# Two early batches as six rows on each of 96 partitions, cast by the load queue, with q transposed on TensorE for batch 0 and by DMA for batch 1

## The chip, the cores and the metric

The kernel runs on one core of one Trainium2 chip. The metric is device time in microseconds (us), and lower is better. Profiles are of one execution; their times count from the start of its span, which is about 1.7 us shorter than the device time of the same execution.

## The reference

```python
# q, k, v: fp32, 8 batches x 8 heads x 576 rows x 64;  w_in 512 x 2048, w_out 2048 x 512
kv  = einsum('bhsd,bhse->bhde', k, v)
o   = einsum('bhsd,bhde->bhse', q, kv)
o   = o / sqrt(mean(o*o, -1) + 1e-6) * g_norm
x   = o.transpose(0, 2, 1, 3).reshape(4608, 512)
h   = x @ w_in
out = (h * sigmoid(1.702 * h)) @ w_out          # fp32
```

## The kernel before

The kernel runs in stages, one dense tile each. Stage t does the dense part of batch t (a hidden half with w_in, then a projection half with w_out) and, in between its matmuls, the attention of batch t + 1. The last stage does the 64 left-over rows of all batches. Units of attention work hang at numbered steps: of 16 groups of the hidden half and of 64 matmuls of the projection half. TensorE takes everything in program order, so a unit that waits holds all that follow: in the profile after, no matmul ran from 42.08 to 46.41 while one `out` waited.

For one batch and each of four pairs of heads: `kv` forms k^T v; q has to come transposed; `out` multiplies it with kv; `ss` sums the squares and `apply` scales. Batches 0 and 1 are special because nothing has been loaded yet. In the kernel before they lie as nine rows on each of 64 partitions and head, two heads stacked, are loaded as fp32 on SyncE's queue (v: cast by GpSimd's), and are cast by three engines into zero-filled block-diagonal tiles. TensorE transposes q with a stacked identity:

```python
def early_load(n, b, c):                       # q and k, fp32
    nc.sync.dma_start(out=staged[b][n][:, c, :], in_=early_src(n, b, c))

class Early(Attention):                        # batches 0 and 1
    def kv(self, c):
        ...
        for j in range(NJ):                    # NJ = 9, zeros in half of kz
            nc.tensor.matmul(t, kz[:, c, j, :], v9[:, c, j * D : (j + 1) * D],
                             start=(j == 0), stop=(j == NJ - 1))
    def q(self, c):
        for j in range(NJ - 1):
            nc.tensor.matmul(t[:, j * R : (j + 1) * R], qz[:, c, j, :], stack, ...)
        nc.vector.tensor_copy(s, t)
...
load_w_in(4, 8); load_w_in(8, 16)              # GpSimd's queue, cast on the way
load_w_out(0, 8); load_w_out(8, 12)
early_load_v(1, 0, 4)
ask_after(0, w_out_sb[:, 7, 0:1])              # batch 1's q and k only when w_out(0, 8) is there
early_stage(1)
for c in range(NPAIR):
    for n in "kq":
        early_load(n, 1, c)
...
# stage 0, projection half, pair c of batch 1
s0 = 14 + 9 * c
at2(s0 - 6, second_casts, c); at2(s0, of(1, "kv", c)); at2(s0 + 2, of(1, "q", c))
at2(s0 + 8, of(1, "out", c)); at2(s0 + 13, of(1, "ss", c)); at2(s0 + 13, of(1, "apply", c))
```

Batches 2 to 7 come in another layout; their q is already transposed by DMA (`qTd`, 512 rows, and `qTr`, the rest), issued from SyncE.

## Time and profile before

| | before |
|---|---|
| device time, median (all its runs) | 301.28 us (299.9 to 302.7) |
| span of the profile | 300.3 us |
| stage 0 begins (hidden half) | 18.85 |
| stage 0, projection half begins | 34.82 |
| stage 1 begins | 53.89 |
| stage 2 begins | 85.92 |
| one later stage | 30.81 |
| granted clock | 1.00 from 7.06 us on; no entry before |

Where the trace has no entry for the clock, the views print 1.00. The head shows that this is no reading: the 12 filler matmuls (matmuls that compute nothing) before 6.5 us step 0.427 us and last up to 634 ns each, those after 8.96 us step 0.22 us and last 379 ns. So TensorE began at about half speed. The lines by stage, and why stages and not busy shares are read, are in the prediction below.

### The profile page before, as it was taken

How to read it: one execution, taken by the hardware profiler on the slowest of the kernel's cores; microseconds unless marked ns; L12 is line 12 of the kernel's file. 1: busy time of each engine (PE TensorE's matmuls, PEld its weight loads, DVE VectorE, ACT ScalarE, POOL GpSimd, SP SyncE). 2: the span in 40 equal slices, each digit the busy share in tenths (PEclk: the TensorE clock that was granted, in tenths of full speed). 3: DMA queues.
4: the chain of work that ended last, by engine and by line, in shares of the span. 5: the costliest groups of instructions: out<-in, count | busy, mean ns of one | idle time of the engine just before them, and what ended most of it. 6: DMA issues, size and time to landing. Idle time of an engine off the chain costs nothing.

```text
span 300.3 us, 3952 instructions
## 1 busy us (share of the span) xinstructions
PE 287.3 (96%) x1549; PEld 135.1 (45%) x1549; DVE 98.0 (33%) x201; ACT 184.0 (61%) x293; POOL 28.7 (10%) x52
## 2 busy tenths in 40 slices
PE   7689989999999999999999999999999999999993
PEld 2334445454445444544444444444454444444441
DVE  5552056262370055214531444134512400110020
ACT  7578757867766775677567756685758666016400
POOL 5550070020012002002000200000000000000000
PEclk9999999999999999999999999999999999999999
DMA  6999994978999992694179507000700030012033
GB/s 144 286 168 196 230 309 145 323 179 238 311 346 252 207 331 101 159 360 87 49 181 326 137 2 219 0 0 2 213 5 2 1 140 2 0 52 87 2 70 70
DMA packets 52531, 44.56 MB, mean 148 GB/s; under 512 B 25120, under 2 KB 47648, under 8 KB 51744
## 3 DMA queue, kind: packets, MB, share of 16 engines
q1 hardware_dynamic: 47584, 38.94, 45.2%
q0 software_dynamic: 4768, 5.37, 11.0%
q8 instruction: 12, 0.20, 0.3%
q14 instruction: 7, 0.06, 0.1%
q10 hardware_dynamic: 160, 0.00, 0.0%
HBM read 36.70 MB, written 9.44 MB: 154 GB/s over the span
## 4 chain that ended last, share of the span: by engine, by line
PE 74%; DMA 18%; DVE 3%; POOL 1%; SPq 1%; issue 1%; ACT 0%; POOLq 0%; DVEq 0%
PE o L369 37%; PE hT L328 30%; DMA qf<-in_q_dram 7%; DMA w_out_sb<-in_moe_w_out_dram 5%; DMA qTd<-qbuf 4%; PE ss L261 2%; DMA kf<-in_k_dram 2%; PE outT L233 2%; PE kvp L202 1%; SPq L93 1%; DVE qbuf L139 0%; DVE kbuf L139 0%; DVE kbuf L101 0%; DVE vbuf L143 0%; POOL kbuf L101 0%
## 5 line engine op out<-in xcount | busy, mean ns | idle before, releaser
L369 PE MATMUL o<-w_out_sb,gT 128*128 128x512 f16 x576 | 137.9, 379 | 0.0
L337 ACT ACTIVATE gT<-hT 128x512 f16<-128x512 f32 x142 | 84.6, 599 | 69.5 <-PE hT L328 69.3
L328 PE MATMUL hT<-xT,w_in_sb 128*128 128x512 f16 x504 | 115.5, 379 | 0.6 <-DVE xT L271 0.5
L369 PEld LDWEIGHTS <-gT 128*128 128x128 f16 x576 | 55.3, 98 | 65.0 <-issue 2.3
L328 PEld LDWEIGHTS <-w_in_sb 128*128 128x128 f16 x576 | 55.2, 98 | 63.3 <-issue 2.2
L271 DVE SCALAR_TENSOR_TENSOR xT<-outT,g_col,rs 128x512 f16<-128x512 f32 x32 | 24.0, 750 | 66.1 <-ACT rs L265 66.1
L377 DVE COPY osb<-o 128x512 f32<-128x512 f32 x34 | 23.3, 685 | 60.7 <-PE o L369 60.7
L263 ACT ACTIVATE ln<-ss,eps_t 128x512 f32<-128x512 f32 (+1 forms) x40 | 25.9, 647 | 18.8 <-PE ss L261 18.7
L265 ACT ACTIVATE rs<-ln 128x512 f32<-128x512 f32 (+1 forms) x40 | 23.5, 589 | 1.3
L253 ACT ACTIVATE sq<-outT 128x512 f16<-128x512 f32 (+1 forms) x40 | 21.7, 542 | 1.7 <-PE outT L233 1.5
L214 DVE CAST kvb<-kvp 64x256 f16<-64x256 f32 x12 | 5.1, 422 | 36.5 <-PE kvp L210 36.4
L261 PE MATMUL ss<-sq,ones 128*128 128x512 f16 (+1 forms) x40 | 14.3, 357 | 0.8 <-ACT sq L253 0.6
L145 POOL CAST krem<-krf 64x512 f16<-64x512 f32 x6 | 4.0, 659 | 112.8 <-DMA krf<-in_k_dram 89.4
L328 PE MATMUL hT<-x_rem,w_in_sb 128*128 128x512 f16 x64 | 14.0, 379 | 0.0
L139 DVE CAST qbuf<-qf 128x512 f16<-128x512 f32 x24 | 10.5, 439 | 2.5 <-DMA qf<-in_q_dram 2.5
L421 PE MATMUL idle<-kvb 128*128 128x512 f16 x29 | 10.1, 483 | 1.2 <-DVE kvb L160 1.2
L139 DVE CAST kbuf<-kf 128x512 f16<-128x512 f32 x24 | 10.5, 438 | 0.0
L337 ACT ACT_TABLE_LOAD x8 | 10.3, 1283 | 0.1
L143 DVE CAST vbuf<-vf 128x512 f16<-128x512 f32 x24 | 10.3, 431 | 0.0
L202 PEld LDWEIGHTS <-kbuf 128*128 128x128 f16 x96 | 7.4, 98 | 5.7
L275 DVE SCALAR_TENSOR_TENSOR x_rem<-outT,g_col,rs 128x256 f16<-128x256 f32 x8 | 3.9, 484 | 17.9 <-ACT rs L265 17.9
L233 PE MATMUL outT<-qTd,kvb 128*128 128x512 f16 x24 | 9.1, 379 | 0.4 <-DMA qTd<-qbuf 0.3
(53 smaller groups left out, 117.9 us busy)
## 6 DMA issues: line engine op xcount, KB each, us to landing
kf<-in_k_dram SPq DMA_DIRECT2D x6, 1024.0 KB, 5.8
vf<-in_v_dram SPq DMA_DIRECT2D x6, 1024.0 KB, 8.8
qf<-in_q_dram SPq DMA_DIRECT2D x6, 1024.0 KB, 11.9
out_dram<-osb SPq DMA_DIRECT2D x6, 1024.0 KB, 3.9
kf<-in_k_dram SPq DMA_DIRECT2D x8, 288.0 KB, 7.2
qf<-in_q_dram SPq DMA_DIRECT2D x8, 288.0 KB, 6.9
out_dram<-osb SPq DMA_DIRECT2D x4, 512.0 KB, 6.0
w_in_sb<-in_moe_w_in_dram POOLq DMA_DIRECT2D x2, 512.0 KB, 6.1
```

The costliest lines, as they stand in the source:

```text
L139: nc.vector.tensor_copy(out=dst[:, c, :, :].rearrange("p j (l d) -> p j l d", l=2), in_=src[n][:, h, :].rearrange("p l (j d) -> p j l d", ...
L202: nc.tensor.matmul(t[:, c, :].rearrange("p (l d) -> p l d", l=2), kh[:, c, j, :], vh[:, 2 * c : 2 * c + 2, j * D : (j + 1) * D], start=(j ...
L233: nc.tensor.matmul(t.rearrange("p c r -> p (c r)"), self.kb[:, c, :], self.qT[c][:, 0:SM], start=True, stop=True,)
L253: nc.scalar.activation(sq[:, 0:n], t, AFT.Square)
L261: nc.tensor.matmul(t[:, 0:n], ones2, sq[:, 0:n], start=True, stop=True)
L263: nc.scalar.activation(ln[:, 0:n], t[:, 0:n], AFT.Ln, bias=eps_t, scale=1.0 / D)
L265: nc.scalar.activation(rs[:, 0:n], ln[:, 0:n], AFT.Exp, bias=0.0, scale=-0.5)
L271: nc.vector.scalar_tensor_tensor(self.x[:, c, :], o, g_col, rs, op0=ALU.mult, op1=ALU.mult)
L328: nc.tensor.matmul(h, w_in_sb[:, ko, fo * P : (fo + 1) * P], x[:, ko, :], start=(ko == 0), stop=(ko == KO - 1),)
L337: nc.scalar.activation(gT[:, fo, :], h, AFT.Gelu_apprx_sigmoid)
L369: nc.tensor.matmul(os[mo], gT[:, fo, mo * P : (mo + 1) * P], w_out_sb[:, fo, :], start=(fo == 0), stop=(fo == FO - 1),)
L377: (nc.scalar.copy if deep and mo % 2 else nc.vector.tensor_copy)(osb[:, mo, :], os[mo])
```

## The change

The intent: spare the zero fills and the casts of the early batches by letting the load queue cast, spare TensorE work by packing two heads side by side in the array (64-column tiles, batch 0) or in one 128-column matmul (batch 1), and take batch 1's q off TensorE by a DMA transpose. The diff, cut to its core:

```diff
-    def early_load(n, b, c):
-        nc.sync.dma_start(out=staged[b][n][:, c, :], in_=early_src(n, b, c))
+    def early_load(n, b, c0, c1):                     # q, k, v; PE_ = 96, NJ = 6
+        nc.gpsimd.dma_start(
+            out=raw[n][0:PE_, c0:c1, :].rearrange("p c (l x) -> p (c l) x", l=2),
+            in_=early_src(n, b, c0, c1),
+        )
 ...
-        for c in range(NPAIR):                        # casts of batches 2 to 7
-            for n, dst in (("k", kh), ("q", qh)): ...
-            nc.vector.tensor_copy(out=vh[:, h, :], in_=src["v"][:, h, :])
+        for n, dst in (("q", qh), ("k", kh), ("v", vh)):
+            for c in range(NPAIR): ...
 ...
-    class Early(Attention):
+    class First(Attention):
         def kv(self, c):
+            for j in range(NJ):
+                for hl in range(2):
+                    nc.tensor.matmul(t[hl * D : (hl + 1) * D, :],
+                                     kraw[0:PE_, c, x], vbuf[0:PE_, c, x], ...)
         def q(self, c):
+            for j in range(NJ):
+                for hl in range(2):
+                    nc.tensor.transpose(t[hl * D : (hl + 1) * D, j * PE_ : (j + 1) * PE_],
+                                        qraw[0:PE_, c, ...], ident[0:PE_, 0:PE_])
+    class Second(Attention):
+        def transpose_q(self):
+            s = attn.tile([P, NPAIR * NJ, PE_], F16, name="qTe", tag="qTe", bufs=1)
+            nc.sync.dma_start_transpose(out=s, in_=qbuf[0:PE_, :])
 ...
     load_w_in(8, 16)
     load_w_out(0, 8)
+    early_load("q", 1, 0, 4)
+    early_load("k", 1, 0, 4)
+    early_load("v", 1, 0, 4)
     load_w_out(8, 12)
-    early_load_v(1, 0, 4)
-    ask_after(0, w_out_sb[:, 7, 0:1])
-    ... batch 1's q and k on SyncE's queue ...
+    load_w_out(12, 16)
 ...
+            at1(14, of(1, "pack_q"))
+            at1(14, of(1, "transpose_q"))
             for c in range(NPAIR):
-                ... (casts, kv, q, out, ss, apply at 14 + 9 * c and after)
+                at2(6, of(1, "pack_k", c))
+                at2(18 + c, of(1, "kv", c))
+                at2(27 + 8 * c, of(1, "out", c))
+                at2(34 + 8 * c, of(1, "ss", c))
+                at2(34 + 8 * c, of(1, "apply", c))
```

Not shown: q and k of batch 0's first pair still come as fp32 on SyncE's queue; 8 filler matmuls (matmuls that compute nothing) open the head instead of 12; the output of batches 0 and 1 is stored in eight pieces instead of two; kv of later batches comes one group later.

More of the change, by code (lines that the diff above doesn't have):

```diff
@@ L6 @@
 from concourse._compat import with_exitstack
-from concourse.masks import make_identity
 F16 = mybir.dt.float16
@@ L42 @@
     NT = B + 1
-    NJ = S // R
     EARLY = 2
+    PE_ = 96
+    NJ = S // PE_
+    assert PE_ * NJ == S and PE_ % 32 == 0
     const = ctx.enter_context(tc.tile_pool(name="const", bufs=1))
@@ L66 @@
     qbuf = const.tile([P, NPAIR * NJ * P], F16)
-    vbuf = const.tile([P, NPAIR * NJ * D], F16)
+    kraw = const.tile([P, NPAIR, 2 * NJ * D], F16)
+    qraw = const.tile([P, NPAIR, 2 * NJ * D], F16)
+    vbuf = const.tile([P, NPAIR, 2 * NJ * D], F16)
     ident = const.tile([P, P], F16)
-    stack = const.tile([P, D], F16)
     ones2 = const.tile([P, P], F16)
     eps_t = const.tile([P, 1], F32)
-    zero_t = const.tile([P, 1], F16)
     g_col = const.tile([P, 1], F32)
@@ L76, with early_src, pack @@
     x_rem = const.tile([P, KO, B * R], F16)
-    kz = kbuf.rearrange("p (c j e) -> p c j e", c=NPAIR, j=NJ)
-    qz = qbuf.rearrange("p (c j e) -> p c j e", c=NPAIR, j=NJ)
-    v9 = vbuf.rearrange("p (c x) -> p c x", c=NPAIR)
-    def early_stage(b):
-        staged[b] = {
-            n: stage.tile([P, NPAIR, NJ * D], F32, name=f"{n}f", tag=f"{n}f") for n in "kq"
-        }
-    def early_src(n, b, c):
-        return srcs[n][b, 2 * c : 2 * c + 2].rearrange("l (p j) d -> (l p) (j d)", j=NJ)
-    def early_load(n, b, c):
-        nc.sync.dma_start(out=staged[b][n][:, c, :], in_=early_src(n, b, c))
-    def early_load_v(b, c0, c1):
-        src = v[b, 2 * c0 : 2 * c1].rearrange("(c l) (p j) d -> (l p) c (j d)", l=2, j=NJ)
-        nc.gpsimd.dma_start(out=v9[:, c0:c1, :], in_=src)
-    def early_cast(b, c, n, hl, copy):
-        r = slice(hl * D, (hl + 1) * D)
-        copy(
-            out=(kz if n == "k" else qz)[r, c, :, r],
-            in_=staged[b][n][r, c, :].rearrange("p (j d) -> p j d", d=D),
+    raw = {"k": kraw, "q": qraw, "v": vbuf}
+    def early_src(n, b, c0, c1):
+        return srcs[n][b, 2 * c0 : 2 * c1].rearrange("h (p j) d -> p h (j d)", j=NJ)
+    def early_load(n, b, c0, c1):
[3 more added lines that the diff above has]
+        )
+    def pack(n, dst, c):
+        nc.vector.tensor_copy(
+            out=dst[0:PE_, c * NJ * P : (c + 1) * NJ * P].rearrange(
+                "p (j l d) -> p j l d", j=NJ, l=2
+            ),
+            in_=raw[n][0:PE_, c, :].rearrange("p (l j d) -> p j l d", l=2, j=NJ),
         )
@@ L108 @@
     qh = qbuf[:, 0 : NPAIR * SM].rearrange("p (c j e) -> p c j e", c=NPAIR, j=J)
-    vh = vbuf[:, 0 : NPAIR * SM].rearrange("p (h x) -> p h x", h=H)
+    vh = vbuf.rearrange("p c x -> p (c x)")[:, 0 : NPAIR * SM].rearrange("p (h x) -> p h x", h=H)
     def load_batch(b):
@@ L113, in load_batch @@
         for n in "kvq":
-            if n == "v":
-                t = stage.tile([P, NPAIR * SM], F32, name="vf", tag="vf")
-            else:
-                t = stage.tile([P, NPAIR, NJ * D], F32, name=f"{n}f", tag=f"{n}f")
-                t = t.rearrange("p c x -> p (c x)")[:, 0 : NPAIR * SM]
-            t = tiles[n] = t.rearrange("p (h x) -> p h x", h=H)
+            t = tiles[n] = stage.tile([P, H, J * D], F32, name=f"{n}f", tag=f"{n}f")
             nc.sync.dma_start(
@@ L135, in casts @@
         src = staged[b]
-        for c in range(NPAIR):
-            h = slice(2 * c, 2 * c + 2)
-            for n, dst in (("k", kh), ("q", qh)):
-                nc.vector.tensor_copy(
-                    out=dst[:, c, :, :].rearrange("p j (l d) -> p j l d", l=2),
-                    in_=src[n][:, h, :].rearrange("p l (j d) -> p j l d", j=J),
-                )
-            nc.vector.tensor_copy(out=vh[:, h, :], in_=src["v"][:, h, :])
+        for n, dst in (("q", qh), ("k", kh), ("v", vh)):
+            for c in range(NPAIR):
+                h = slice(2 * c, 2 * c + 2)
+                if n == "v":
+                    nc.vector.tensor_copy(out=vh[:, h, :], in_=src["v"][:, h, :])
+                else:
+                    nc.vector.tensor_copy(
+                        out=dst[:, c, :, :].rearrange("p j (l d) -> p j l d", l=2),
+                        in_=src[n][:, h, :].rearrange("p l (j d) -> p j l d", j=J),
+                    )
@@ L144, in casts @@
         for n, t in (("kr", krem[b % 2][0:R]), ("vr", vrem[b % 2][0:R]), ("qr", qrem[b % 2])):
             nc.gpsimd.tensor_copy(out=t.rearrange("p c (l d) -> p (c l) d", l=2), in_=src[n])
+    first = {}
+    for n in "qk":
+        first[n] = stage.tile([P, H, J * D], F32, name=f"{n}f", tag=f"{n}f")
+        first[n] = first[n].rearrange("p h x -> p (h x)")[0:PE_, 0 : 2 * NJ * D]
+        nc.sync.dma_start(
+            out=first[n].rearrange("p (h x) -> p h x", h=2), in_=early_src(n, 0, 0, 1)
+        )
@@ L148 @@
     for hl in range(2):
         nc.scalar.dma_start(out=g_col[hl * D : (hl + 1) * D, :], in_=g_norm.unsqueeze(1))
-    early_stage(0)
-    for c in range(NPAIR):
-        for n in "kq":
-            early_load(n, 0, c)
-    early_load_v(0, 0, 1)
-    early_load_v(0, 1, 2)
-    make_identity(nc, ident)
-    early_load_v(0, 2, 4)
-    nc.vector.memset(zero_t, 0.0)
-    nc.vector.memset(kvb[1], 0.0)
-    nc.scalar.preload_act_table_set("natural_log_exp_and_others")
-    for c in range(NPAIR):
-        nc.vector.memset(kz[:, c], 0.0)
-        nc.scalar.copy(
-            qz[:, c].rearrange("p j e -> p (j e)"), zero_t.to_broadcast([P, NJ * P])
-        )
-        if c == 0:
-            nc.vector.memset(ones2, 0.0)
-            nc.vector.memset(ones2[0:D, 0:D], 1.0)
-            nc.vector.memset(ones2[D:P, D:P], 1.0)
-            nc.vector.tensor_add(stack, ident[:, 0:D], ident[:, D:P])
-            nc.vector.memset(eps_t, EPS)
@@ L173 @@
-    nc.vector.memset(kvb[0], 0.0)
+    nc.vector.memset(ident, 0.0)
+    nc.vector.memset(kvb[1], 0.0)
+    early_load("v", 0, 0, 1)
+    nc.gpsimd.affine_select(
+        out=ident,
+        in_=ident,
+        compare_op=ALU.not_equal,
+        fill=1.0,
+        base=0,
+        pattern=[[-1, P]],
+        channel_multiplier=1,
+    )
+    for c in range(1, NPAIR):
+        for n in "qkv":
+            early_load(n, 0, c, c + 1)
+    nc.scalar.preload_act_table_set("natural_log_exp_and_others")
@@ L176, in load_w_in @@
+    nc.vector.memset(ones2, 0.0)
+    nc.vector.memset(ones2[0:D, 0:D], 1.0)
+    nc.vector.memset(ones2[D:P, D:P], 1.0)
+    nc.vector.memset(eps_t, EPS)
     def load_w_in(f0, f1):
@@ L211, in kv, with keep_kv @@
             if c == NPAIR - 1:
-                for hl in range(2):
-                    r = slice(hl * D, (hl + 1) * D)
-                    nc.vector.tensor_copy(self.kb[r, :, r], t[r, :, r])
+                self.keep_kv()
+        def keep_kv(self):
+            for hl in range(2):
+                r = slice(hl * D, (hl + 1) * D)
+                nc.vector.tensor_copy(self.kb[r, :, r], self.kvp[r, :, r])
         def transpose_q(self):
@@ L282, in apply @@
                 )
-    class Early(Attention):
+    class First(Attention):
         def kv(self, c):
-            pool, tag = (ps_o, "o") if self.b == 0 else (ps_a, "att")
-            t = pool.tile([P, D], F32, name="kv9", tag=tag)
+            t = ps_o.tile([P, D], F32, name="kv0", tag="o")
             for j in range(NJ):
-                nc.tensor.matmul(
-                    t,
-                    kz[:, c, j, :],
-                    v9[:, c, j * D : (j + 1) * D],
-                    start=(j == 0),
-                    stop=(j == NJ - 1),
-                )
+                for hl in range(2):
+                    x = slice((hl * NJ + j) * D, (hl * NJ + j + 1) * D)
+                    nc.tensor.matmul(
+                        t[hl * D : (hl + 1) * D, :],
+                        kraw[0:PE_, c, x],
+                        vbuf[0:PE_, c, x],
+                        start=(j == 0),
+                        stop=(j == NJ - 1),
+                    )
             nc.vector.tensor_mul(
@@ L302, in q @@
         def q(self, c):
-            t = ps_h.tile([P, SM], F32, name="q9", tag="hT")
-            for j in range(NJ - 1):
-                nc.tensor.matmul(
-                    t[:, j * R : (j + 1) * R], qz[:, c, j, :], stack, start=True, stop=True
-                )
-            s = attn.tile([P, SM], F16, name="qT", tag="qT", bufs=4)
+            t = ps_h.tile([P, S], F16, name="q0", tag="hT")
+            for j in range(NJ):
+                for hl in range(2):
+                    nc.tensor.transpose(
+                        t[hl * D : (hl + 1) * D, j * PE_ : (j + 1) * PE_],
+                        qraw[0:PE_, c, (hl * NJ + j) * D : (hl * NJ + j + 1) * D],
+                        ident[0:PE_, 0:PE_],
+                    )
@@ L309, in q, with rest, pack_q, pack_k @@
+            s = attn.tile([P, S], F16, name="qT", tag="qT", bufs=4)
             nc.vector.tensor_copy(s, t)
             self.qT[c] = s
-        def q_rest(self):
-            t = ps_a.tile([P, NPAIR, R], F32, name="q9r", tag="att")
+        def rest(self, c):
+            return self.qT[c][:, SM:S]
+    class Second(Attention):
+        def pack_q(self):
             for c in range(NPAIR):
-                nc.tensor.matmul(t[:, c, :], qz[:, c, NJ - 1, :], stack, start=True, stop=True)
-            self.qr = attn.tile([P, NPAIR, R], F16, name="qrT", tag="qrT", bufs=1)
-            nc.vector.tensor_copy(self.qr, t)
+                pack("q", qbuf, c)
+        def pack_k(self, c):
+            pack("k", kbuf, c)
+        def kv(self, c):
+            if c == 0:
+                self.kvp = ps_a.tile([P, NPAIR, P], F32, name="kvp", tag="att")
+            t = self.kvp
+            v2 = vbuf[0:PE_, c, :].rearrange("p (l x) -> p l x", l=2)
+            for j in range(NJ):
+                nc.tensor.matmul(
+                    t[:, c, :].rearrange("p (l d) -> p l d", l=2),
+                    kbuf[0:PE_, (c * NJ + j) * P : (c * NJ + j + 1) * P],
+                    v2[:, :, j * D : (j + 1) * D],
+                    start=(j == 0),
+                    stop=(j == NJ - 1),
+                )
+            if c == NPAIR - 1:
+                self.keep_kv()
+        def transpose_q(self):
+            s = attn.tile([P, NPAIR * NJ, PE_], F16, name="qTe", tag="qTe", bufs=1)
+            nc.sync.dma_start_transpose(out=s, in_=qbuf[0:PE_, :])
+            s = s.rearrange("p (c j) r -> p c (j r)", c=NPAIR)
+            for c in range(NPAIR):
+                self.qT[c] = s[:, c, 0:SM]
+            self.qTe = s
@@ L319, in rest @@
         def rest(self, c):
-            return self.qr[:, c, :]
+            return self.qTe[:, c, SM:S]
     def dense(t, units1, units2, group, deep):
@@ L381, in project @@
                         if 2 * mo + g < EARLY:
-                            rows = rows.rearrange("(p j) m -> p j m", j=NJ)[:, NJ - 1, :]
+                            p0 = SM % PE_
+                            rows = rows[bass.DynSlice(NJ * p0 + SM // PE_, R, step=NJ), :]
                         else:
@@ L395, in dense @@
         if t < EARLY:
-            rows = out[t * S : (t + 1) * S, :].rearrange("(p j) m -> p j m", j=NJ)
-            for g in range(2):
+            n = 0
+            while n < SM:
+                mo, j, p = n // P, n // PE_, n % PE_
+                m = min((mo + 1) * P, (j + 1) * PE_) - n
                 nc.sync.dma_start(
-                    out=rows[:, bass.DynSlice(g, NPAIR, step=2), :],
-                    in_=osb[g * R : (g + 1) * R, :, :],
+                    out=out[t * S : (t + 1) * S, :][bass.DynSlice(NJ * p + j, m, step=NJ), :],
+                    in_=osb[n % P : n % P + m, mo, :],
                 )
+                n += m
         elif t < B:
@@ L405, in dense @@
             )
-    a0 = Early(0)
-    def first_casts(c):
-        early_cast(0, c, "k", 0, nc.vector.tensor_copy)
-        early_cast(0, c, "k", 1, nc.gpsimd.tensor_copy)
-        early_cast(0, c, "q", 0, nc.vector.tensor_copy if c == 3 else nc.gpsimd.tensor_copy)
-        early_cast(0, c, "q", 1, nc.gpsimd.tensor_copy if c == 2 else nc.scalar.copy)
+    a0 = First(0)
+    nc.scalar.copy(qraw[0:PE_, 0, :], first["q"])
+    nc.vector.tensor_copy(kraw[0:PE_, 0, :], first["k"])
     idle_ps = ps_h.tile([P, SM], F32, name="idle", tag="hT")
@@ L427, in busy @@
             )
-    first_casts(0)
-    busy(12)
+    busy(8)
     for c in range(NPAIR):
+        a0.q(c)
         a0.kv(c)
-        a0.q(c)
         if c:
             a0.ss(c - 1)
-        if c == 1:
-            load_w_in(0, 4)
-        if c + 1 < NPAIR:
-            first_casts(c + 1)
         busy(2)
@@ L445 @@
             busy(3)
+    load_w_in(0, 4)
     load_w_in(4, 8)
@@ L448 @@
     load_w_out(0, 8)
+    early_load("q", 1, 0, 4)
+    early_load("k", 1, 0, 4)
+    early_load("v", 1, 0, 4)
     load_w_out(8, 12)
-    early_load_v(1, 0, 4)
-    after = const.tile([P, 2], F32)
-    def ask_after(i, landed):
-        nc.gpsimd.tensor_copy(after[:, i : i + 1], landed)
-        nc.sync.dma_start(out=after[0:D, i : i + 1], in_=g_norm.unsqueeze(1))
-    ask_after(0, w_out_sb[:, 7, 0:1])
-    early_stage(1)
-    for c in range(NPAIR):
-        for n in "kq":
-            early_load(n, 1, c)
-    def second_casts(c):
-        early_cast(1, c, "k", 0, nc.vector.tensor_copy)
-        early_cast(1, c, "k", 1, nc.gpsimd.tensor_copy)
-        early_cast(1, c, "q", 0, nc.gpsimd.tensor_copy)
-        early_cast(1, c, "q", 1, nc.scalar.copy)
-        if c == 0:
-            load_w_out(12, 16)
+    load_w_out(12, 16)
+    after = const.tile([1, 1], F32)
     def third():
-        ask_after(1, w_out_sb[:, FO - 1, 0:1])
+        nc.gpsimd.tensor_copy(after, w_out_sb[0:1, FO - 1, 0:1])
+        nc.sync.dma_start(out=after, in_=g_norm[0:1].unsqueeze(1))
         load_batch(2)
@@ L479, in start @@
     def start(b):
-        live[b] = Early(b) if b < EARLY else Attention(b)
+        live[b] = Second(b) if b == 1 else Attention(b)
     for t in range(NT):
@@ L497 @@
             at1(("ko", 1), of(0, "apply", NPAIR - 1))
-            at1(4, of(0, "q_rest"))
-            at1(6, of(0, "out", NPAIR))
+            at1(4, of(0, "out", NPAIR))
             at2(4, of(0, "ss", NPAIR, True))
@@ L504 @@
                 at1(8, nc.vector.memset, r[R:P], 0.0)
+            at1(14, of(1, "pack_q"))
+            at1(14, of(1, "transpose_q"))
             for c in range(NPAIR):
-                s0 = 14 + 9 * c
-                at2(s0 - 6, second_casts, c)
-                at2(s0, of(1, "kv", c))
-                at2(s0 + 2, of(1, "q", c))
-                at2(s0 + 8, of(1, "out", c))
-                at2(s0 + 13, of(1, "ss", c))
-                at2(s0 + 13, of(1, "apply", c))
-            at2(s0, third)
+                at2(6, of(1, "pack_k", c))
[3 more added lines that the diff above has]
+                at2(34 + 8 * c, of(1, "apply", c))
+            at2(14, third)
         elif b < B:
             if t == 1:
-                at1(3, of(1, "q_rest"))
                 at2(46, of(1, "out", NPAIR))
@@ L526 @@
             for c in range(NPAIR):
-                at1((11 if t == 1 else 8) + c, of(b, "kv", c))
+                at1((11 if t == 1 else 9) + c, of(b, "kv", c))
             for c in range(NPAIR + 1):
```

## The prediction

> **What bounds the kernel now.** I read the shares first, then the table by stage, then the chain of waits, and last the DMA rate in short stretches. One core is in use and the granted clock is 1.00 throughout, so clock plays no part.
>
> ```profile
> PE 287.3 (96%) x1549; PEld 135.1 (45%) x1549; DVE 98.0 (33%) x201; ACT 184.0 (61%) x293; POOL 28.7 (10%) x52
> ```
>
> TensorE looks full, but a 128x512 matmul counts 379 ns busy while a run of them steps much faster (in the chain, 64 take 13.81 us, so 0.216 us each). Holes under 0.16 us are therefore hidden, and filler matmuls (10.1 us in the head) count as work. So I time stages by their boundaries: from 18.85 (first dense matmul), 34.82, 53.89, 85.92, 117.00 on.
>
> ```profile
> 18.85:34.82 15.97, 14.95 (x75) 6.68 (x74) 3.01 (x7) 12.99 (x22) 0.53 (x2) 1.00 1.18 202
> 34.82:53.89 19.07, 17.80 (x142) 9.00 (x141) 9.94 (x18) 13.18 (x21) 6.21 (x10) 1.00 0.83 242
> 53.89:85.92 32.03, 31.72 (x172) 15.09 (x171) 13.16 (x26) 23.23 (x39) 3.76 (x6) 1.00 0.99 268
> 85.92:117.00 31.08, 30.97 (x163) 14.63 (x161) 10.84 (x23) 20.75 (x34) 3.03 (x6) 1.00 0.94 241
> 117.00:147.81 30.81, 30.81 (x163) 14.65 (x161) 10.84 (x23) 20.64 (x33) 1.51 (x3) 1.00 0.59 169
> ```
>
> Columns: stretch, length, busy time of PE, weight load, DVE, ACT, POOL, clock, DMA share, GB/s. Steady state is 30.81: 128 dense matmuls (27.63) and 3.18 of attention for the next batch. From 117.00 to the end nothing can be gained. The head, stage 0 (19 + 35 us) and stages 1 and 2 hold everything: what can move is the moment at which stage 2 begins, 85.92, plus its 0.27 us hole. What sets 85.92 is in the chain of waits:
>
> ```profile
> 3.19 10.09 DMA qf<-in_q_dram
> ...
> 16.80 14.95 DMA w_out_sb<-in_moe_w_out_dram
> ...
> 32.70 5.97 DMA kf<-in_k_dram
> ...
> 49.13 11.93 DMA qf<-in_q_dram
> ...
> 65.66 4.39 DMA qTd<-qbuf
> 70.09 0.38 PE outT L233
> ```
>
> Start, length, what. Until 70.09 the chain is nearly all DMA; TensorE takes over only there. By 46.9, when the last of w_out lands, the queues have read three tensors twice (8x8x576x64 fp32 = 3.54 MB a batch) and two weights of 4.19 MB, 15.47 MB: 344 GB/s from 2 us on. How far that is from what the engines can do:
>
> ```profile
> 2.00:7.00 5.00, 4.52 (x11) 1.46 (x10) 2.83 (x9) 4.99 (x5) 2.96 (x6) 1.00 0.81 182
> 16.00:18.00 2.00, 1.69 (x21) 1.00 (x21) 2.00 (x4) 1.92 (x4) 2.00 (x4) 1.00 0.66 69
> 26.00:34.00 8.00, 8.00 (x43) 3.68 (x41) 1.05 (x4) 5.80 (x11) 0.19 (x1) 1.00 1.23 205
> 37.00:42.00 5.00, 3.73 (x33) 1.76 (x31) 2.79 (x5) 2.17 (x4) 3.04 (x5) 1.00 1.03 397
> 42.00:47.00 5.00, 5.00 (x54) 2.80 (x53) 3.29 (x8) 3.84 (x7) 2.98 (x5) 1.00 0.75 128
> 66.80:70.00 3.20, 3.00 (x22) 1.54 (x21) 0.84 (x2) 1.79 (x3) 0.00 (x0) 1.00 0.96 184
> ```
>
> GB/s counts bytes written, so a casting load at 205 reads 410. Full rate is about 400 read (26 to 34; uncast 397 at 37 to 42). The first five microseconds, 16 to 18 (weights asked for late, GpSimd being busy with casts) and 42 to 47 run below it.
>
> [...]
>
> **The change part by part.**
> Head. Zero fills (4 DVE at 0.54, 4 ACT at 1.15 us) and batch 0's 16 casts go, except one ACT and one DVE copy of pair 0. kv costs 12 small matmuls a pair in place of 9, q 12 in place of 8; both were about 0.25 us. None of this bounds: pairs arrive at the pace of DMA, 0.885 MB each, 2.3 us at 385. I take 385 for 1536-byte rows, between 348 for 1024-byte rows (50 to 59 us) and 400. Reading from 2.0 on, [...] batch 0 ends at [...] 11.9; before, the last q landed at 13.28. GpSimd no longer casts, so weights follow with no hole: w_in and half of w_out, 6.29 MB at 405, 15.5 us, end 27.4; before, 31.75. TensorE: first dense matmul near 15.5 instead of 18.85 (when the first 1 MB of w_in lands), projection from about 31 instead of 34.82.
> Batch 1 loads. 3.54 MB at 385, 9.2 us. Into the same stretch falls the new transpose of 96x3072 f16, 0.59 MB. The old pair of transposes, likewise 0.59 MB, took most of 66.8 to 70 (0.96 x 3.2 = 3.1 us of all engines); I take 2.75. v lands last: 27.4 + 9.2 + 2.75 [...] = 40.1. TensorE reaches its place, projection step 18, at 31 + 18 x 0.216 = 34.9, and waits about 5 us, where it now waits 1.27 before kv.
> From there: 46 steps (9.93), kv 24 x 0.055 = 1.3, four out and four ss, 1.7: stage 1 begins 13.0 after v, at 53.1 (53.89 before). Removed from TensorE in stages 0 and 1: kv 1.04 + q 0.96 + rest of q 0.28, less 1.3 for the new kv, so 1.0 us.
> Stage 1. The rest of w_out, 2.1 MB at 405, ends 5.2 us after v, 45.3 (46.9 before). Batch 2 is requested behind it and follows the old pattern (46.9 to q landed at 61.06, 14.2): 59.5. But casts now run q, k, v. Transposes gain: they start after 4 casts, not 11. kv loses: it needs 9 casts before its first pair, at 0.335 each plus about 1 us of the slowing seen at 61.8 to 63.9 (0.84 instead of 0.42): 4.0, so kv at 63.5. By its own path TensorE reaches it at 53.1 + 3.5 (grouped part) + 8 x 0.863 = 63.5: both arrive together. Then 5 hidden groups and kv (5.35), 64 projections with out and ss (16.0): stage 2 at 84.9 instead of 85.92.
> Stage 2. Earlier transposes remove its 0.27 hole. The eight output pieces instead of two cost SyncE queue time that I expect to be covered.
> Sum: -1.0 (stage 2's start) - 0.27 = -1.3: 300.0. I shade it to 299.6, because each lag that the two paths share (385 against a possible 410 for batch loads) errs on the slow side.
>
> **The rivals.**
> (a) TensorE sets the pace, and its savings count in full: head 3.3, the wait before kv 1.3, holes of stage 0 (1.1), stage 1 (0.9), work 1.0: up to 7 us, 294. For it: the page's 96%. Against it: the chain, DMA until 70; the same bytes have to be read. It would need batch 2's q landed before 55; 15.47 MB at 405 alone ends at 40.2 from 2.0, and 14.2 more is 54.4, with no start, latency or transpose. I give it 4%.
> (b) Nothing gained: the new transpose eats what the closed holes give (2.75 against about 4), batch 2's q lands at 61 as before, and kv, now behind 9 casts, starts at 65.1 instead of 64.64: 301.5. [...] For it: DMA stays saturated. Against: slack at 16 to 18 and 42 to 47 is real.
> (c) Batch loads run at 410 and the transpose hides in gaps: v at 37, stage 2 near 82.5: 297.5.
> (d) Requests from GpSimd, 96-row tiles [...] run slower than 385, say 330: each batch costs 1.5 us more, 302.5. Nine requests at 0.75 us feed 0.295 MB each, 393 GB/s, so there is little to spare at the start.
>
> **Range and chances.** Between (b) and (c) lies most of it: 297.2 to 301.5 holds 8 in 10, centre 299.6. Two per cent faster is 295.3 or less, only through (a): 0.04. Slower by over 2% is above 307, for which several of (d) and the clock must meet: 0.02. Within 2%: 0.94.
>
> **What would show it right or wrong.** In the changed kernel's chain: DMA of batch 1's v, then of batch 2's q or its casts, ahead of TensorE. First dense matmul at 15 to 16. TensorE waiting 3 to 6 us at kvp in stage 0, on the DMA of v. Bytes read near 400 GB/s from 4 to 27 us without a hole. The table by stage: stage 2 begins at 84 to 86, all later stages 30.81. I am wrong if v lands before 36, if the transpose takes little from the loads, if the wait at step 18 lowers the granted clock, or if stage 2 shows a longer wait for its transpose because eight output pieces hold SyncE's queue.

Two terms of its sum go with that, an allowance for the start of the loads and one for their landing: what is left of it, 2.0 + 9.2 for batch 0, 15.5 for the weights, 9.2 + 2.75 for batch 1, puts v at 38.65, where the author's sum came to 40.1 and went on from there to 300.0, shaded to 299.6. The 330 of rival (d) is a supposition, not a reading. That GB/s counts bytes written is seen in the page of before: GpSimd's casting loads read 10.7 MB of fp32 and stand there with 5.37 MB (q0).

## More of the kernel before

The kernel before took 299.9 to 302.7 us over all its runs here, so differences of a few tenths are read from stage lengths in a profile and not from one time.

## The result, and the profile after

The changed kernel is correct and slower: 306.42 us median (306.17 to 306.66, four runs) against 301.59 (301.13 to 302.17) for the kernel before in the same session. The ratio is 1.0159, interval 1.0137 to 1.0181. The predicted range, 297.2 to 301.5, missed it.

The table by stage of the changed kernel, with the columns of the table in the prediction (stretch, length, busy time of PE, weight load, DVE, ACT, POOL, clock, DMA share, GB/s):

```profile
16.48:32.22 15.74, 14.85 (x72) 6.57 (x72) 2.59 (x6) 12.75 (x22) 3.50 (x5) 1.00 1.22 207
32.22:58.81 26.59, 20.23 (x99) 8.98 (x97) 6.41 (x15) 10.09 (x17) 0.38 (x2) 0.87 1.11 229
58.81:90.54 31.73, 31.51 (x168) 14.93 (x167) 11.97 (x25) 23.46 (x39) 2.97 (x6) 1.00 1.01 273
90.54:121.30 30.76, 30.76 (x163) 14.59 (x161) 11.86 (x23) 20.71 (x34) 3.58 (x6) 1.00 0.67 173
```

Stage by stage against the table of before: the head is 2.37 us shorter (16.48 against 18.85), the hidden half of stage 0 0.23 shorter, stage 1 0.30 and stage 2 0.3 shorter. One half-stage is 7.52 longer: the projection half of stage 0, 26.59 instead of 19.07. Of the stages in the table it is also the only one whose clock is not 1.00. The whole loss sits there. What TensorE waited for, in us in total, times, longest:

```profile
PE outT L231 <- DMA qTe<-qbuf: 4.3, 1, 4.3
PE kvp L335 <- DMA vbuf<-in_v_dram: 2.0, 1, 2.0
```

And the chain of waits of the changed kernel there (start, length, what):

```profile
17.70 15.94 DMA vbuf<-in_v_dram
33.64 12.64 DMA qTe<-qbuf
46.41 0.58 PE outT L231
46.99 2.99 PE o L403 x7
```

The new transpose of batch 1's q was issued at 33.64 and landed at 46.27. TensorE came to the first `out` of batch 1 at about 42 and stood until 46.41. Then seven projection matmuls took 2.99 us where seven take 1.51 elsewhere. The clock explains that; here are three single microseconds of the changed kernel, in the same columns:

```profile
44.00:45.00 1.00, 0.00 (x0) 0.00 (x0) 0.00 (x0) 0.00 (x0) 0.00 (x0) 0.96 1.27 108
47.00:48.00 1.00, 1.00 (x3) 0.29 (x2) 0.00 (x0) 0.60 (x1) 0.00 (x0) 0.50 0.67 178
51.00:52.00 1.00, 1.00 (x4) 0.39 (x3) 0.17 (x1) 0.97 (x3) 0.00 (x0) 0.62 1.09 366
```

TensorE idles, the granted clock (third number from the end) falls to 0.50 at 44.93, and it is 1.00 again only from 51.76 on. The first line holds a second fact: at 44 to 45 the DMA engines are fully busy (1.27) but write only 108 GB/s. So why did 0.59 MB take 12.6 us? The share of each DMA queue from 40 to 42 (queue, packets, MB written, share of 16 engines; q0 is GpSimd's queue with the casting loads, q1 SyncE's with the transpose):

```profile
q0 software_dynamic: 308, 0.31, 90.8%
q1 hardware_dynamic: 308, 0.08, 29.6%
```

The packet counts are equal. A load packet writes 1 KB (2 KB of fp32 read), a transpose packet 256 B, and so the transpose gets a fifth of the bytes. From 45 to 46, when the loads are through, it gets 615 packets in one microsecond.

These equal turns are seen from 37.6 to 42.5 only, 5 of the 12.6 us. From its issue at 33.64 until 37.60 no transpose packet moved at all. And from 42.5 to 45, with few load packets left, the transpose still crept. The queues from 44 to 45:

```profile
q1 hardware_dynamic: 399, 0.10, 123.0%
q0 software_dynamic: 7, 0.01, 3.7%
```

That is 49 ns of an engine a packet (1.23 x 16 us over 399) where it took 31 ns in the turns and 18 ns from 45 on, after the last load packet had ended at 44.72. Why it crept, and why it started so late, no run shows. Without the loads both are much shorter: in `e1_quiet` the first packet came 1.3 us after the issue, and only 35.0 to 35.5 was slow (112 packets).

The half-stage adds up so: 64 projection matmuls 13.81, rest of batch 0's ss 0.11, kv 24 x 0.055 = 1.32, four out 0.86, four ss 0.86, together 16.96. The wait for v is 2.2 by the pitch of 0.216 (the views count a matmul as busy for 379 ns where a run steps by 216, hence 2.0), the one for the transpose 4.5. That leaves 26.59 - 16.96 - 6.7 = 2.9, mostly the clock.

### The profile page after: what moved, and what is told of

The parts are those of the page before. It is cut to its first block, busy times and chain, and to the rows that moved or that the text cites. A ratio compares the mean times of both kernels' runs of the same rounds, so it can differ in the third digit from the quotient of the medians.

```text
span 304.8 us, 3833 instructions
## 1 busy us (share of the span) xinstructions
PE 288.7 (95%) x1521; PEld 134.1 (44%) x1521; DVE 87.7 (29%) x187; ACT 175.2 (57%) x283; POOL 23.9 (8%) x43
## 4 chain that ended last, share of the span: by engine, by line
PE 84%; DMA 11%; ACT 2%; DVE 1%; issue 1%; POOL 0%; POOLq 0%
PE o L403 39%; PE hT L362 36%; DMA vbuf<-in_v_dram 7%; DMA qTe<-qbuf 4%; PE ss L259 3%; PE outT L231 2%; PE kvp L197 2%; PE idle L456 1%; ACT ln L261 1%; ACT rs L263 1%; PE kvp L205 0%; PE hO L362 0%; PE q L307 0%; ACT osb L411 0%; PE outT L242 0%
## 5 line engine op out<-in xcount | busy, mean ns | idle before, releaser
L403 PE MATMUL o<-w_out_sb,gT 128*128 128x512 f16 x576 | 139.4, 383 | 0.0
L403 PEld LDWEIGHTS <-gT 128*128 128x128 f16 x576 | 56.2, 99 | 67.4 <-issue 4.9
L212 DVE CAST kvb<-kvp 64x256 f16<-64x256 f32 x14 | 5.9, 422 | 50.1 <-PE kvp L205 46.1
L456 PE MATMUL idle<-kvb 128*128 128x512 f16 x25 | 9.1, 492 | 1.3 <-DVE kvb L149 1.3
L131 DVE CAST kbuf<-kf 128x512 f16<-128x512 f32 x24 | 9.6, 460 | 0.0
L197 PE MATMUL kvp<-vbuf,kbuf 128*128 128x128 f16 x96 | 9.3, 219 | 0.0
L129 DVE CAST vbuf<-vf 128x512 f16<-128x512 f32 x24 | 8.5, 416 | 0.0
```

The costliest lines, as they stand in the source:

```text
L197: nc.tensor.matmul(t[:, c, :].rearrange("p (l d) -> p l d", l=2), kh[:, c, j, :], vh[:, 2 * c : 2 * c + 2, j * D : (j + 1) * D], start=(j ...
L403: nc.tensor.matmul(os[mo], gT[:, fo, mo * P : (mo + 1) * P], w_out_sb[:, fo, :], start=(fo == 0), stop=(fo == FO - 1),)
L456: nc.tensor.matmul(idle_ps, kvb[1][:, 0, :], kvb[1].rearrange("p c r -> p (c r)"), start=True, stop=True,)
```

## The experiments

Theory A: the transpose is not slow, it starves beside the casting loads, which share the engines with it packet by packet; its wait brings the half clock with it. Theory B: the transpose is slow in itself (96 rows, 3072 columns, or SyncE's 8.07 us of issuing it). Theory C: something else in the change costs (96-row loads, small tiles, output pieces).

**The transpose with the engines to itself** (`e1_quiet`). The k and v of batch 1 and the last half of w_out are asked for after it has landed.

```diff
     early_load("q", 1, 0, 4)
-    early_load("k", 1, 0, 4)
-    early_load("v", 1, 0, 4)
-    load_w_out(8, 12)
-    load_w_out(12, 16)
+    def rest_of_loads():                      # called right after transpose_q
+        nc.gpsimd.tensor_copy(landed, live[1].qTe[0:1, 0, 0:1])
+        ... the four loads ...
```

> The changed kernel, but k and v of batch 1 and the last half of w_out are asked for only when the transpose of q has landed, so the transpose has the DMA engines to itself. Theory A (the transpose starves behind the casting loads of GpSimd's queue): it lands 4 to 6 us after its issue, like the transposes of later batches (5.4), instead of 12.6. Theory B (96 rows or 3072 columns are slow as such, or SyncE's 8 us of issuing them): 11 to 13 us again. The total gets longer in both, 308 to 313, because 4.5 MB of loads come later; it is not the point.

Measured: 311.51 us, one run. The transpose's own lines in this run (issue: duration in ns and start; then us from issue to landing):

```profile
L347 SPq DMA_TRANSPOSE qTe<-qbuf x1: 3785/3785/3785, 33.0 to 33.0; - x1
DMA to landing us min/median/max: 5.1/5.1/5.1
```

It lands in 5.1 us instead of 12.6, with the same rows, columns and engine, and SyncE issues it in 3.79 us instead of 8.07: the long issue went with the loads beside it. B falls. The rest of the loads then came too late (10.4 us of waiting for v), as intended.

**Filler in the hole** (`e2_fill`).

```diff
+            at2(27, fill, 20)     # 20 matmuls into a spare PSUM tile, ahead of out(1, 0)
```

> The changed kernel with 20 useless matmuls (20 x 0.216 = 4.3 us) put just before the first out of batch 1, in the hole in which TensorE waits for the transpose. The wait itself stays: the transpose lands at 46.3 as before. Theory: the half clock from 45 to 51.4 follows from the idle time and costs about 2.5 us beside the wait's 4.3: with the hole filled the clock stays 1.00 and the time is 303.6 to 304.2. Rival (the clock falls for another reason, or the loads and not TensorE set the end): 306.4.

Measured: 304.13 us (303.87 to 304.55), ratio to before 1.0100 (1.0062 to 1.0138). The same kind of single microseconds as above:

```profile
44.00:45.00 1.00, 1.00 (x7) 0.47 (x5) 0.00 (x0) 0.00 (x0) 0.00 (x0) 1.00 1.27 80
47.00:48.00 1.00, 1.00 (x7) 0.41 (x6) 0.00 (x0) 0.49 (x1) 0.00 (x0) 1.00 0.45 144
```

The transpose landed at 46.3 as before, 12.8 us after its issue. The clock stays at 1.00, seven matmuls run in the microsecond from 47 instead of three, and the span falls from 304.8 to 302.4. So of the loss 2.3 to 2.4 us is the clock that follows the wait, got back by work that computes nothing.

**q of batch 1 asked for earlier** (`e4_q_early`).

```diff
+    early_load("q", 1, 0, 4)
     load_w_out(0, 8)
-    early_load("q", 1, 0, 4)
```

> The changed kernel with batch 1's q asked for before the first half of w_out, so its transpose is issued about 5 us earlier, near 28.5. Theory A, starving until the casting queue is empty near 43: it still lands at 44 to 46, the wait shrinks by 0 to 2 us, 304 to 306.5. Theory B, a fixed 12.6 us: it lands at 41, no wait at out, no half clock, 299 to 300.

Measured: 304.89 us (304.60 to 305.48), ratio to before 1.0126 (1.0087 to 1.0165). Waits of TensorE, and the transpose's time to landing:

```profile
PE kvp L335 <- DMA vbuf<-in_v_dram: 5.1, 1, 5.1
PE outT L231 <- DMA qTe<-qbuf: 0.4, 1, 0.4
```

```profile
DMA to landing us min/median/max: 18.7/18.7/18.7
```

Issued at 29.0 instead of 33.6, the transpose landed at 47.7 instead of 46.3. A fixed duration of 12.6 is refuted once more. The wait moved: beside the transpose the loads fell from about 205 GB/s written to 145 to 155, and from 38.0 to 38.5 both queues all but stood (32 GB/s); v came at 42.4, not 38.6. I had expected the wait to stay at `out`; the time lay in the range, the place did not.

**q of batch 1 on TensorE** (`e3_te_q`), straight from the cast rows as for batch 0.

```diff
-            at1(14, of(1, "pack_q"))
-            at1(14, of(1, "transpose_q"))
+            q = First.q; rest = First.rest            # in class Second
             for c in range(NPAIR):
-                at2(6, of(1, "pack_k", c))
+                at2(5 + 3 * c, of(1, "q", c))
+                at2(16, of(1, "pack_k", c))
```

> The changed kernel with batch 1's q transposed on TensorE as batch 0's is, straight from the cast rows (48 small matmuls, about 1.2 us), so no DMA transpose in stage 0. If the transpose is the whole loss: no wait at out, no half clock, v lands near 38 and TensorE waits 1 to 2 us there, stage 2 begins at 82 to 84, 297 to 299. If something else in the change costs (96-row loads, small tiles, output pieces, order of casts): above 301.

Measured: 300.77 us (300.49 to 300.94), ratio to before 0.9987 (0.9942 to 1.0031): 5.65 us faster than the changed kernel in the medians, level with the kernel before. The longest waits of TensorE:

```profile
PE kv L290 <- DMA vbuf<-in_v_dram: 1.7, 1, 1.7
PE q L307 <- DVE qT L313: 1.3, 1, 1.3
```

No wait for a transpose, none for v of batch 1, clock 1.00 throughout stage 0, stage 2 at 84.63. It is slower than the 297 to 299 expected, because of the second line, a wait that I made: the copy of the first q out of PSUM stood on VectorE behind batch 0's last `apply`. C is refuted as the cause of the loss: the rest of the change, all of it still in, is no slower than before.

**The same with q's groups moved** (`e6_q_placed`), at steps 1, 3, 12 and 15.

```diff
-                at2(5 + 3 * c, of(1, "q", c))
+                at2((1, 3, 12, 15)[c], of(1, "q", c))
```

> Batch 1's q on TensorE, with its four groups of transposes at projection steps 1, 3, 12 and 15 in place of 5, 8, 11 and 14. In the run before, the second group waited 1.27 us for the first one's copy, which stood on VectorE behind batch 0's last apply. With the first two copies ahead of it that wait goes: stage 2 begins 1.0 to 1.3 us earlier, 299.3 to 300.0. Rival, v of batch 1 now lands too late and takes over the wait: 300.5.

Measured: 299.34 us (299.19 to 299.52), ratio to before 0.9939 (0.9906 to 0.9973). Stage 2 begins at 83.30; the waits of TensorE from 20.5 us on are gone but for 0.2. This is the fastest version. Run again in five rounds (`e6_again`, same kernel):

> The fastest version so far once more, in the same rounds as the one above, to place it against the kernel before: 0.6% faster, 299.1 to 299.8.

Measured: 299.98 us (299.83 to 300.98), ratio 0.9967 (0.9944 to 0.9990). That is just above the 299.8 expected. So it beats both kernels, by 0.3 to 0.6% the kernel before. In the profile of this repeat TensorE waited 1.8 us for the first part of w_in, which it had not done in the first; loads vary by that much from run to run.

**Four transposes instead of one** (`e5_split`), each a pair's 768 columns.

```diff
-            nc.sync.dma_start_transpose(out=s, in_=qbuf[0:PE_, :])
+            for c in range(NPAIR):
+                nc.sync.dma_start_transpose(
+                    out=s[:, c * NJ : (c + 1) * NJ, :],
+                    in_=qbuf[0:PE_, c * NJ * P : (c + 1) * NJ * P])
```

> The changed kernel with batch 1's q transposed by four DMA requests, one a pair, in place of one. In the trace of the changed kernel, packets of the two queues alternate one for one (308 and 308 in two microseconds), a transpose packet carrying 256 B and a load packet about 1 KB written. If that stays, 0.17 MB of transposes are through by 42, so pair 0 (0.15 MB) lands near 41, in time for its out at 42.1, and the others near 43.5, 44.5 and 46, each about when its out comes (8 steps apart): no long wait, clock 1.00, 299 to 301. Rival, the transposes as a whole land only when the casting queue is empty: pair 0 lands after 44, wait over 2 us, 303 to 306.

Measured: 301.77 us (300.36 to 302.24), ratio to before 1.0004 (0.9957 to 1.0051). The waits of TensorE have no line for the transpose. The two longest are:

```profile
PE kvp L335 <- DMA vbuf<-in_v_dram: 2.4, 1, 2.4
PE kv L290 <- DMA vbuf<-in_v_dram: 2.1, 1, 2.1
```

The same bytes at the same alternation (315 transpose packets to 313 of loads from 40 to 42), but the first pair is usable when it is needed. That repairs nearly all of the loss with three more requests. The time is a little above my range: here the wait for v, 2.4 us, already brought the clock to 0.50 from 40 to 43.

**The last half of w_out held back** (`e9_w_out_held`) until the transpose has landed.

```diff
-    load_w_out(8, 12)
-    load_w_out(12, 16)
+    def rest_of_loads():                      # called right after transpose_q
+        nc.gpsimd.tensor_copy(landed, live[1].qTe[0:1, 0, 0:1])
+        load_w_out(8, 12); load_w_out(12, 16)
```

> The changed kernel, but the last two requests for w_out (2.1 MB read) wait on GpSimd until the transpose has landed. If the alternation of packets starves the transpose, it runs alone from about 38.5 on, when v has landed, and lands at 41 to 42 instead of 46.3; out then waits under 0.5 us. The price: w_out's third quarter lands near 45 where step 32 wants it at 43.2. Clock near 1.00, 300 to 302.5. If the transpose lands at 45 or later all the same, the alternation is not what holds it.

Measured: 304.32 us (303.77 to 304.52), ratio to before 1.0102 (1.0066 to 1.0137). The queue of the transpose from 38 to 40, and TensorE's longest wait:

```profile
q1 hardware_dynamic: 1838, 0.46, 104.1%
```

```profile
PE o L403 <- DMA w_out_sb<-in_moe_w_out_dram: 3.5, 1, 3.5
```

With the loads gone the transpose moves 1838 packets in 2 us instead of 314 and lands at 40.4, 7.0 us after its issue; `out` did not wait. That part of the expectation held. The price was double what I had reckoned: the engines stood empty from 40 to 42 and were about half busy until 43 before w_out flowed again, so TensorE waited 3.5 us for it, and the clock fell to 0.50 at 47.4, a microsecond after the wait had ended. The total missed its range of 300 to 302.5.

**Smaller load packets** (`e11_small_packets`): the last half of w_out in halves of 256 columns.

```diff
-    load_w_out(8, 12)
-    load_w_out(12, 16)
+    ... for f0 in (8, 12), for n0 in (0, 256): the same rows, columns n0 to n0 + 256
```

> The changed kernel with the last half of w_out asked for in halves of 256 columns, so that the rows the transpose competes with carry 512 B written (1 KB read) in place of 1 KB (2 KB), twice as many of them. If the engines alternate packet by packet, the counts of the two queues stay one for one while both have work (39 to 43), but each load packet is done sooner: the transpose gets 400 to 480 packets in 2 us in place of 314, 0.10 to 0.12 MB in place of 0.08, and the loads fall from 0.31 to 0.20 to 0.24 MB written. If the engines shared by bytes or by time, or the transpose were held at 157 packets a microsecond by something of its own, its count would stay near 314. The landing (46.3) and the total (305 to 308) need not move: there are more packets to get past.

Measured: 307.06 us, one run. The queues from 40 to 42, to be read against the 308 and 308 of the changed kernel:

```profile
q0 software_dynamic: 492, 0.24, 88.2%
q1 hardware_dynamic: 490, 0.13, 46.8%
```

Still one for one, and the transpose's share rose with the shorter packets of its rival, from 0.08 to 0.13 MB, a little more than expected, though nothing about the transpose was changed. That settles for these runs how the engines share while both queues have work: by turns of packets (308 to 308, 492 to 490), not by bytes or time. It landed after 13.5 us. I take that to be because there were now more packets to get past; again none of its packets moved in the first 4.0 us.

**A warmer head** (`e7_warm`): the version of `e6_q_placed` with 16 fillers.

```diff
-    busy(8)
+    busy(16)
```

> The same with 16 filler matmuls ahead of batch 0 in place of 8, so that TensorE is idle for under 1 us before pair 0's kv, where it was idle 2.0 us and the clock then stood at 0.50 from 7 to 10.6. If the head counts: clock 1.00 in the head, first dense matmul near 15.5 instead of 16.5, 298.3 to 299.0. Rival, the head is not what sets the end (v of batch 1 or w_in lands as before and the gain turns into a wait): within 0.3 of the run without it.

Measured: 300.10 us (299.48 to 300.82), ratio to before 0.9965 (0.9926 to 1.0004). The clock was 1.00 from 4.2 us on and TensorE reached its first dense matmul about 1 us earlier, at 15.5. There it waited:

```profile
PE kvp L335 <- DMA vbuf<-in_v_dram: 1.0, 1, 1.0
PE hT L362 <- DMA w_in_sb<-in_moe_w_in_dram: 0.8, 1, 0.8
```

The rival was right in kind: the gain of the head became waits for w_in and v. The head does not set the end, the loads do. In time it missed: the run is 0.8 us above `e6_q_placed` of the same rounds, where the rival allowed 0.3. The head that the expectation describes is the changed kernel's; in `e6_q_placed` the fillers ran at the slow step until 10.15 us.

**More loads in the first microseconds** (`e10_best`): pair 1's q and k also as fp32 on SyncE's queue, 16 fillers, and batch 1's kv, out and ss four steps later.

```diff
-                at2(18 + c, of(1, "kv", c))
-                at2(27 + 8 * c, of(1, "out", c))
+                at2(22 + c, of(1, "kv", c))
+                at2(31 + 8 * c, of(1, "out", c))      # ss, apply likewise; loads and casts of pair 1 not shown
```

> Batch 1's q on TensorE and 16 filler matmuls, as in the run with the warm head, and two moves against the waits that it showed (w_in 0.8, v of batch 1 1.0): pair 1's q and k of batch 0 also come as fp32 over SyncE's queue, to fill the first 6 us in which the engines ran at half rate, and batch 1's kv, out and ss come four steps later. If DMA supply from the first microseconds on is what bounds: w_in and v land 0.7 to 1.5 us earlier, no wait at kv, stage 2 begins at 81.5 to 82.8, 297.5 to 299. Rival, the queue of GpSimd starts no earlier and total reads stay: v at 38.5 as before, later kv alone hides its wait, 299 to 299.6.

Measured: 300.47 us (300.23 to 300.80), ratio to before 0.9977 (0.9955 to 0.9999), no better than `e6_again` in the same rounds, and above both expected ranges. (The half rate in the expectation: from 2 to 6 us the changed kernel wrote 0.57 MB uncast and 0.16 MB cast, so read 0.89 MB, 222 GB/s, against 410 at 34 to 36.) v of pair 0 came later: its first use was at 8.60, in `e6_again` at 6.99. TensorE also waited 0.75 us for ScalarE's copy of pair 1's q, which this run adds. So the first dense matmul came at 17.42, just when the wait for w_in had let it come in `e6_again`, and stage 2 began at 84.28, not at 81.5 to 82.8. I take the later v for the same sharing between queues that hurt the transpose; no run tests it.

**The order of the casts alone** (`e8_order_alone`): the kernel before with this part only.

```diff
-        for c in range(NPAIR):                 # k, q, v of a pair, then the next pair
+        for n, dst in (("q", qh), ("k", kh), ("v", vh)):
+            for c in range(NPAIR): ...
-                at1((11 if t == 1 else 8) + c, of(b, "kv", c))
+                at1((11 if t == 1 else 9) + c, of(b, "kv", c))
```

> The kernel before with one part of the change alone: batches 2 to 7 cast all of q, then k, then v, and kv one group later. My reading: stage 2's hole of 0.27 us goes because the transposes start earlier, so stage 2 takes 30.8 instead of 31.08; in stage 1, batch 2's kv has to wait for nine casts where it waited for none, 0 to 1 us more. Total within 0.5 of before. Rival: the order of the casts brings the change's 0.3 us in stage 1 too.

Measured: 300.33 us, one run. In the chain of waits, the beginnings of stages 2 and 3:

```profile
84.49 8.63 PE hT L330 x40
115.29 8.63 PE hT L330 x40
```

Stage 2 takes 30.80 instead of 31.08, as in the changed kernel, so this part brings that. Stage 1 took 31.6 instead of 32.03, as the rival had it; the wait for nine casts that I feared did not occur. One profile each shows it. The single time, 0.9 below the session's median of the kernel before where I had said within 0.5, proves nothing.

## Why the prediction was wrong, point by point

- **The step that failed** is in "Batch 1 loads": "Into the same stretch falls the new transpose of 96x3072 f16 ... I take 2.75", added to the loads, after which v "lands last". The bytes were sound, and 2.75 is not far from what moving takes alone (3.3 us from first packet to last in `e1_quiet`). The sharing was not: I let the loads pay for the transpose. In fact the transpose paid: it had 12.64 us from issue to landing instead of 5.1 alone. v landed earlier than predicted (kv at 38.63, not 40.1), and the transpose last, at 46.27. "If the transpose takes little from the loads" was among the prediction's own signs of being wrong.
- **What hung on it**: "stage 1 begins 13.0 after v" had no wait between kv and `out`. It began 20.2 us after v: the wait of 4.5, the half clock of 2.4 by the filler run, and some 0.3 of other holes make the 7.2.
- **The clock**: it was among the prediction's own signs of being wrong, but at step 18, for a wait of about 5 us there. That wait was 2.0 and the clock held. It fell nine steps later. The length of a wait alone does not sort the cases: waits of 2.43 us (`e5_split`, kvp) and 2.02 (head of the changed kernel) were followed by 0.50, others of 2.04 (changed kernel, kvp) and 2.22 (`e9_w_out_held`, kvp) left it at 1.00. In the changed kernel the clock changed at 7.38, 10.80, 44.93 and 51.76, which lie 3.41 us, ten times and twice that apart; whether the place of a wait against such points decides, no run tests. That the clock was "1.00 throughout" before is wrong for the head (see the table of before), which, by the warm head's run, does not set the end.
- **How queues share was not asked.** I reckoned with one sum of bytes for all queues. The traces show turns by packet: 308 to 308 in the changed kernel, with smaller load packets 492 to 490. A hint stood in the profile of before, where the two queues moved 164 and 155 packets from 6 to 8 us and 195 and 179 from 8 to 10; that the engines take turns was not shown by it. From such turns, and 256 B in a transpose packet against 1 KB written in a load's, it follows that the transpose is held up. How long does not: an estimate with the measured 154 packets a microsecond gives 15 us for its 2304 if the loads lasted, and the 12.6 were made up otherwise (3.9 us of nothing, 5 of turns, the rest faster).
- **The profile of before held a warning.** The transpose of batch 3 took 8.15 us (from 93.20) where that of batch 2 took 4.39. Other traffic filled the engines at the time; no run here took that transpose apart.
- **Right in mechanism**: the head (first dense matmul predicted near 15.5, measured 16.48; the clock stood at 0.50 from 7.38 to 10.80 after 2.0 us of idle), the projection half (31 and 32.22), w_out's end (45.3 and 45.1: the sum of the bytes was right, their order was not), stage 2's hole (gone). The head's gain did not count, as (a)'s counter-argument said and the warm head showed.
- **Wrong but harmless**: 385 GB/s for 1536-byte rows. From 34 to 36 these loads wrote 205 GB/s, so read 410, like the weights. And kv of batch 2 did not wait for nine casts. A slip: 3.54 MB a batch is three times 8x576x64 fp32, not 8x8x576x64.
- **What the plain sum gives without the failed term**: `e3_te_q` and `e6_q_placed`, which do that transpose on TensorE, took 300.8 and 299.3; the prediction said 299.6. That the rest was near is shown; that each of its terms was, is not, and errors that cancel would be luck.

Open: why no transpose packet at all moved in the first 3.9 us after its issue (1.3 us in `e1_quiet`, without loads), why it crept from 42.5 to 45, and why the same fillers and waits let v or w_in come up to 2 us later in one run than in another.

## What to carry to other kernels

A transfer with small packets beside a busy queue of large ones was not slowed here in proportion to its bytes (308 packets to 308, but 0.08 MB to 0.31): count its packets, and give each the turn of a rival's packet. That was still only part of its delay. If it gates an engine, split it so that the first part lands in time, or do its work elsewhere. And ask of each wait on TensorE whether it can lower the clock, before or after it ends: the wait of 4.3 us here cost 2.4 more after it had ended, which filler got back.
